# The second mixture layer's loop in program order, with the repeats of its first blocks behind it

## The chip, the cores and the metric

The kernel runs on one core of one Trainium2 chip. The metric is the device time of one execution in microseconds (us), of which the median of several runs counts. Five engines run side by side, each with its own queue of instructions: TensorE (PE in the profile, its weight loads PEld), VectorE (DVE), ScalarE (ACT), GpSimd (POOL) and SyncE (SP), which here issues transfers. TensorE's clock has two levels, 1.2 and 2.4 GHz; the profile gives the granted share of full speed.

## What is computed

Sparse attention (the 32 largest scores of each row), then a first mixture layer of dense form (`moe`), then a second one (`moe2`), in which each token goes to one of eight experts:

```python
logits = x @ w_gate + modality_bias[modality_id]
e_idx = np.argmax(logits, axis=1)
...
gate_w = probs[np.arange(N), e_idx]
for e in range(E):
    mask = e_idx == e
    ...
    h = np.maximum(x[mask] @ w1[e], 0.0)
    out[mask] = gate_w[mask, None] * (h @ w2[e])
```

N is 2304 tokens, D 512, F 1024. The change touches the second mixture layer alone.

## The kernel before

*Tiles.* The tokens are sorted by expert into blocks of 128, 18 of them (NBLK) where all blocks are full, with room for 25 (NSLOT). `gather` fetches the 128 rows of a block from device memory by an indirect transfer that GpSimd issues. `blk_x` turns them on TensorE (four transposes into one bank of PSUM, tile px) and splits them into a higher part bxh (ScalarE) and a lower part bxl (VectorE). `mm1` multiplies by the first weight: two halves of 512 columns, 12 matmuls each (three for each of four chunks: higher by higher, lower by higher, higher by lower), and ScalarE writes each half to hid. `blk_h` does for hid what blk_x does for x, in two quarters of four transposes (tiles pht, bhh, bhl). `mm2` has 24 matmuls of 512 columns, three for each of eight chunks; ScalarE scales the result by the gate (bo), and GpSimd issues the indirect transfer that scatters it to the output.

*Weights.* One expert's weights are held at a time, as a higher and a lower part (e1h, e1l; e2h, e2l). `split` makes them from a raw copy: ScalarE the higher parts, VectorE the lower ones, every third chunk by GpSimd (line 1615); four chunks for the first weight, eight for the second. `cond_split` (line 1681) stands before each block of the loop for each weight: it loads a flag from the table `meta` into a register of each queue and, if the block is the first of a new expert, splits the raw copy and loads the next expert's. In this input two experts occur, so each weight is split twice: once for the first expert, and once inside the loop.

*Stages.* The first three blocks (NPRE) are made of the first three sequences' tokens, before the whole routing is known, and run at the end of the first layer. For each of them meta0 says whether the block was not full; then the block is made again with all tokens (`late_block`, with splits where an expert changes). These three repeats stand as tests ahead of the loop (lines 1724 to 1730). The loop (1732) runs over blocks 3 to 17. Behind it stands a test for blocks above 18 (1750), and the test of `missed`, which repeats the whole kernel exactly (1763). In this input none of these bodies is run.

*Order.* The first layer is put in order by a planner of the kernel's own and emitted with a manual schedule. The second layer is left to the framework's scheduler, which orders each engine's instructions by a simulated time line. A test (`tc.If`) is a branch in each engine's queue: a load of the value into a register, a compare-and-branch, and, where the queues join again, waits on events.

*PSUM.* The pool psX holds px, and pht for the first three blocks; psH holds the two halves of mm1; psY two banks for mm2. When the first layer's pool closes, psX2 takes its two banks, both for pht.

Of the kernel before, what the change touches and what calls it, by code (L numbers as in the profile page):

```python
# [151 lines left out]
def moe_chain_kernel(  # L152
# [159 lines left out]
    def whole(redo):  # L312
# [1287 lines left out]
        two = [ep, 1, psX]  # L1600
# [9 lines left out]
        def split(which):  # L1610
            raw, (h, l) = raws[which - 1], (W1, W2)[which - 1]
            n = raw.shape[1]
            for c in range(n):
                A.activation(h[:, c, :], raw[:, c, :], AF.Copy)
                eng = G if c % 3 == 2 else V
                eng.tensor_tensor(l[:, c, :], raw[:, c, :], h[:, c, :].bitcast(F32), op=OP.subtract)
# [10 lines left out]
        def blk_x(i):  # L1627
            xg = XG.pop(i)
            ps = psX.tile([128, NDC, 128], F32, name="px")
            for c in range(NDC):  # L1630
                PE.transpose(ps[:, c, :], xg[:, c * 128:(c + 1) * 128], ident)
            xh = two[0].tile([128, NDC, 128], F32R, name="bxh", bufs=2)
            xl = two[0].tile([128, NDC, 128], F32R, name="bxl", bufs=2)
            A.activation(xh, ps, AF.Copy)  # L1634
            V.tensor_tensor(xl, ps, xh.bitcast(F32), op=OP.subtract)  # L1635
            X[i] = (xh, xl)
# [13 lines left out]
        def blk_h(i):  # L1650
# [3 lines left out]
            for a in range(NF2 // 4):  # L1654
                ps = two[-1].tile([128, 4, 128], F32, name="pht", bufs=two[1])
# [4 lines left out]
            HT[i] = (hh, hl)  # L1660

        def mm2(i):
            hh, hl = HT.pop(i)
            ps = psY.tile([128, DM], F32, name="py")
            seq = [(x, w, c) for c in range(NF2) for x, w in ((hh, W2[0]), (hl, W2[0]), (hh, W2[1]))]
            for n, (x, w, c) in enumerate(seq):
                PE.matmul(ps, x[:, c, :], w[:, c, :], start=(n == 0), stop=(n == len(seq) - 1))  # L1667
# [12 lines left out]

        def cond_split(i, which):
            f = nc.values_load(meta[0:1, 0, i:i + 1], min_val=0, max_val=1)  # L1682
            with tc.If(f > 0):  # L1683
                split(which)
                load_raw(which, e_value(meta[0:1, 1, i:i + 1]))

# [31 lines left out]
        for i in range(NPRE, NPRE + 3):  # L1718
            gather(i)
        raws[1] = mp.tile([128, NF2, DM], F32, name="raw2")  # L1720
        load_raw(1, e_value(meta[0:1, 1, 0:1]))
        load_raw(2, e_value(meta[0:1, 1, 0:1]))
        blk_x(NPRE)
        for i in range(NPRE):
            f = nc.values_load(meta0[0:1, i:i + 1], min_val=0, max_val=1)
            with tc.If(f > 0):
                if i:
                    cond_split(i, 1)
                    cond_split(i, 2)
                late_block(i)  # L1730
        cond_split(NPRE, 1)
        for i in range(NPRE, NBLK):
            if i > NPRE:
                blk_h(i - 1)
# [12 lines left out]
        cond_split(NBLK - 1, 2)  # L1747
        mm2(NBLK - 1)
        more = nc.values_load(meta[0:1, 2, NBLK:NBLK + 1], min_val=0, max_val=NSLOT)  # L1749
        with tc.If(more > NBLK):  # L1750
            for i in range(NBLK, NSLOT):
                nbl = nc.values_load(meta[0:1, 2, i:i + 1], min_val=0, max_val=NSLOT)
                with tc.If(nbl > i):
                    cond_split(i, 1)
                    cond_split(i, 2)
                    late_block(i)
# [3 lines left out]

    whole(False)
    again = nc.values_load(missed, min_val=0, max_val=1)
    with tc.If(again > 0):
# [31 lines left out]
```

## Time and profile before

| | us |
|---|---|
| median of 3 runs | 1018.72 (1018.18 to 1021.07) |
| the profiled execution | 1023.0 |
| its span, first to last instruction | 1021.1 |
| TensorE busy in the span | 924.2 (91%) |
| VectorE busy | 752.5 (74%) |
| ScalarE busy | 699.3 (68%) |
| GpSimd busy | 548.6 (54%) |

The profile is of one execution; its times are counted from the first instruction of the span. The first layer ends at some 765 us, the first three blocks of the second layer at 809.5, and the loop's last matmul starts at 1009.1. A row of the timeline has start, length (merged rows: of all together), engine, line, operation, tiles written and read, and in brackets the idle time of the engine before it with what ended it. An engine's name with a q (PEldq, ACTq) is its queue: loads of registers, branches and event waits, in which the engine itself does nothing. A row of a line's instructions has the count, the shortest, median and longest length in ns, and the first and last start.

### The profile page before, as it was taken

How to read it: one execution, taken by the hardware profiler on the slowest of the kernel's cores; microseconds unless marked ns; L12 is line 12 of the kernel's file. 1: busy time of each engine (PE TensorE's matmuls, PEld its weight loads, DVE VectorE, ACT ScalarE, POOL GpSimd, SP SyncE). 2: the span in 40 equal slices, each digit the busy share in tenths (PEclk: the TensorE clock that was granted, in tenths of full speed). 3: DMA queues.
4: the chain of work that ended last, by engine and by line, in shares of the span. 5: the costliest groups of instructions: out<-in, count | busy, mean ns of one | idle time of the engine just before them, and what ended most of it. 6: DMA issues, size and time to landing. Idle time of an engine off the chain costs nothing. (4 is left out here: it accounts for less than half of the span.)

```text
span 1021.1 us, 21954 instructions
## 1 busy us (share of the span) xinstructions
PE 924.2 (91%) x7518; PEld 769.0 (75%) x7518; DVE 752.5 (74%) x2510; ACT 699.3 (68%) x1624; POOL 548.6 (54%) x831
## 2 busy tenths in 40 slices
PE   5357599999999999999999999998899899989995
PEld 4245478887778888778888887875797678768883
DVE  7999989999999999999989999996327111331110
ACT  7889889899888999888989888765432222432221
POOL 4678568787767786776876776654210211221000
PEclk8568689999999999999999999998899899989998
DMA  7743230132201123000001000000301521241000
GB/s 188 209 133 108 66 95 16 32 92 66 77 14 33 41 46 100 7 17 30 17 20 40 29 10 2 27 1 9 122 13 53 197 63 42 73 157 50 25 22 27
DMA packets 83795, 60.48 MB, mean 59 GB/s; under 512 B 67009, under 2 KB 67009, under 8 KB 83650
## 3 DMA queue, kind: packets, MB, share of 16 engines
q1 hardware_dynamic: 80770, 49.32, 17.0%
q0 software_dynamic: 2880, 9.44, 2.7%
q8 instruction: 65, 1.06, 0.4%
q14 instruction: 80, 0.66, 0.2%
HBM read 49.30 MB, written 9.44 MB: 58 GB/s over the span
## 5 line engine op out<-in xcount | busy, mean ns | idle before, releaser
L828 DVE MAX8 tk<-wk 128x8 f32<-128x288 f32 x576 | 237.2, 446 | 0.0
L876 POOL TENSOR_TENSOR ss<-mk,ss 128x576 f32<-128x576 bf16 x144 | 185.7, 1297 | 45.5 <-ACT mk L874 44.8
L835 DVE MATCH_REPLACE8 wk<-tk,wk 128x288 f32<-128x288 f32 x432 | 188.2, 441 | 0.0
L874 ACT ACTIVATE mk<-ss,kb 128x576 bf16<-128x576 f32 x144 | 110.6, 780 | 19.2 <-POOL kb L777 19.0
L1647 ACT ACTIVATE hid<-ph 128x512 f32<-128x512 f32 x36 | 21.5, 598 | 140.5 <-PE ph L1646 140.5
L882 ACT ACTIVATE ss<-ss,kb 128x576 f32<-128x576 f32 x144 | 112.0, 779 | 2.8 <-POOL ss L876 2.6
L751 PE MATMUL s<-ks,qt 128*128 128x288 f32 x512 | 95.1, 330 | 19.6 <-ACT ss L762 19.6
L762 ACT ACTIVATE ss<-s 128x576 f32<-128x576 f32 x144 | 93.8, 651 | 21.5 <-PE s L751 20.5
L820 DVE TENSOR_TENSOR wk<-s,ss 128x576 f32<-128x576 f32 x144 | 102.7, 744 | 5.6 <-ACT ss L762 5.6
L946 POOL TENSOR_SCALAR ss<-ss,r,nil 128x576 f32<-128x576 f32 x116 | 95.5, 828 | 17.0 <-DVE r L936 12.5
L1671 POOL DMA_INDIRECT out_dram<-bo,tab x18 | 18.3, 1016 | 158.0 <-ACT bo L1670 150.6
L899 PE MATMUL t<-ident,ss 128*128 128x128 f32 x576 | 89.3, 285 | 10.2 <-ACT ss L882 8.9
L1635 DVE TENSOR_TENSOR bxl<-px,bxh 128x512 fp32r<-128x512 f32 x18 | 12.4, 690 | 115.6 <-ACTq L1683 97.5
L751 PEld LDWEIGHTS s<-ks,qt 128*128 128x128 f32 x512 | 78.2, 208 | 23.9 <-ACT ss L762 21.7
L903 ACT ACTIVATE pt<-t 128x512 f32<-128x512 f32 x144 | 84.3, 597 | 12.5 <-PE t L899 11.2
L899 PEld LDWEIGHTS t<-ident,ss 128*128 128x128 f32 x576 | 67.1, 146 | 19.7 <-ACT ss L882 11.7
L967 PE MATMUL m<-pt,v 128*64 128x128 f32 x1024 | 74.8, 291 | 0.0
L967 PEld LDWEIGHTS m<-pt,v 128*64 128x64 f32 x1024 | 58.6, 144 | 11.9 <-issue 11.9
L1088 DVE SCALAR_TENSOR_TENSOR hb<-m,wfac,hb 128x320 f32<-128x320 f32 (+2 forms) x102 | 49.2, 483 | 16.2 <-PE m L1079 14.9
L1646 PE MATMUL ph<-e1h,bxh 128*128 128x512 f32 x144 | 59.5, 413 | 1.2 <-ACT bxh L1634 0.7
L1667 PE MATMUL py<-e2h,bhh 128*128 128x512 f32 x144 | 58.4, 406 | 1.4 <-ACT bhh L1658 1.4
L832 DVE MAX8 tk<-wk 128x8 f32<-128x288 f32 x144 | 58.6, 442 | 0.0
(309 smaller groups left out, 2672.4 us busy)
## 6 DMA issues: line engine op xcount, KB each, us to landing
raw<-in_moe_w_dram SPq DMA_DIRECT2D x6, 2048.0 KB, 9.6
raw<-in_moe_w_dram SPq DMA_DIRECT2D x18, 512.0 KB, 4.1
kraw<-in_v_dram SPq DMA_DIRECT2D x16, 288.0 KB, 3.9
qraw<-in_q_dram SPq DMA_DIRECT2D x64, 64.0 KB, 2.0
kraw<-in_k_dram SPq DMA_DIRECT2D x32, 128.0 KB, 2.6
v<-in_v_dram SPq DMA_DIRECT2D x32, 128.0 KB, 2.7
x_rows<-row SPq DMA_DIRECT2D x16, 256.0 KB, 2.1
raw<-in_moe_w_out_dram SPq DMA_DIRECT2D x6, 512.0 KB, 4.4
```

The lines of the kernel that those rows point to most:

```text
L751: PE.matmul(ST[u][:, hf, t, :HALF], qt[:, i, :], KS[bat(u), p][:, hd, k0:k0 + HALF], start=(n == 0), stop=(n == len(parts) - 1))
L762: A.activation(SS[u][:, :, hf * HALF:(hf + 1) * HALF], ST[u][:, hf, :, :HALF], AF.Copy)
L820: V.tensor_tensor(WK[u][:, :, w, :], ST[u][:, 0, :, :HALF], SS[u][:, :, HALF:S], op=op)
L828: V.max(TK[u][:, t, r * 8:r * 8 + 8], WK[u][:, t, 0, :])
L835: add("DVE", 426, lambda: V.match_replace(WK[u][:, t, 0, :], TK[u][:, t, r * 8:r * 8 + 8], WK[u][:, t, 0, :], NEG), [tk_at(u, (t, r))], [w ...
L874: A.activation(box["m"], SS[u][:, t, :], AF.Relu, bias=KTH[u][:, t, 1:2], scale=-BIG)
L876: add("POOL", 1250, lambda: G.tensor_tensor(SS[u][:, t, :], box["m"], SS[u][:, t, :], op=OP.subtract), [M], rows_at(u, t))
L882: A.activation(SS[u][:, t, :], SS[u][:, t, :], AF.Exp, bias=KTH[u][:, t, 0:1], scale=-scale * UP, accum_out=SUM[u][:, t:t + 1])
L899: PE.transpose(t[:, c, :], SS[u][:, i, c0:c0 + 128], ident)
L903: A.activation(o, box["t"], AF.Copy)
L946: add("POOL", 790, lambda: G.tensor_scalar(SS[u][:, t, :], SS[u][:, t, :], RR[u][:, t:t + 1], nil, op0=OP.mult, op1=OP.add), [at("r", u, N ...
L967: PE.matmul(ps[hd * 64:(hd + 1) * 64, 0, :], vt[:, c, hd, :], PT[u, hd][:, c, :], start=False, stop=(c == KC - 1), skip_group_check=True)
```

## The change

- `split` puts all lower parts on VectorE.
- `blk_x` uses two banks in turn: px in psX and px2 in psX2. pht has one bank instead of two.
- The whole part from the gathers ahead of the loop to the last mm2 is emitted under a manual schedule of all five engines: each engine issues these instructions in program order.
- The loop is written out anew. Each iteration has mm1 of block i, the gather of block i+3, the test for the first weight of i+1, the first half of mm2 of block i-1, the first quarter of blk_h of i, the second half of mm2 of i-1, the second quarter of blk_h, blk_x of i+2, and the test for the second weight of i. A flag loaded for the first weight's test is kept for the second's.
- The three repeats ahead of the loop go behind it, into the test for further blocks, which now asks for either. Ahead of the loop one test is left (meta0 of the third block), which holds splits alone.
- The value of `missed` is loaded in the loop's last iteration.

```diff
-        two = [ep, 1, psX]
+        two, px = [ep, 1, psX], [(psX, "px")]
...
-                eng = G if c % 3 == 2 else V
-                eng.tensor_tensor(l[:, c, :], raw[:, c, :], h[:, c, :].bitcast(F32), op=OP.subtract)
+                V.tensor_tensor(l[:, c, :], raw[:, c, :], h[:, c, :].bitcast(F32), op=OP.subtract)
...
-            ps = psX.tile([128, NDC, 128], F32, name="px")
+            pool, nm = px[i % len(px)]
+            ps = pool.tile([128, NDC, 128], F32, name=nm)
...
-        def blk_h(i):
+        def blk_h(i, between=None):
...
-            for a in range(NF2 // 4):
-                ps = two[-1].tile([128, 4, 128], F32, name="pht", bufs=two[1])
+            HT[i] = (hh, hl)
+
+            def quarter(a):
+                ps = two[-1].tile([128, 4, 128], F32, name="pht")
...
-            HT[i] = (hh, hl)
-
-        def mm2(i):
-            hh, hl = HT.pop(i)
+            for a in range(NF2 // 4):
+                quarter(a)
+                if a == 0 and between:
+                    between()
+
+        def mm2_first(i):
+            hh, hl = HT[i]
...
+            half = len(seq) // 2
+
+            def go(k):
+                for n in range(k * half, (k + 1) * half):
+                    x, w, c = seq[n]
+                    PE.matmul(ps, x[:, c, :], w[:, c, :], start=(n == 0), stop=(n == len(seq) - 1))
+            go(0)
+            return ps, go
+
+        def mm2(i, first=None):
+            ps, go = first or mm2_first(i)
+            go(1)
...
         def cond_split(i, which):
-            f = nc.values_load(meta[0:1, 0, i:i + 1], min_val=0, max_val=1)
+            f = FLAG[i] if i in FLAG else nc.values_load(meta[0:1, 0, i:i + 1], min_val=0, max_val=1)
+            FLAG[i] = f
...
-        blk_x(NPRE)
-        for i in range(NPRE):
-            f = nc.values_load(meta0[0:1, i:i + 1], min_val=0, max_val=1)
-            with tc.If(f > 0):
-                if i:
+        px.append((two[-1], "px2"))
+        E = mybir.EngineType
+        with tc.manual_schedule(engines={E.PE, E.Activation, E.DVE, E.Pool, E.SP}):
+            for i in range(NPRE, NPRE + 3):
+                gather(i)
+            raws[1] = mp.tile([128, NF2, DM], F32, name="raw2")
+            load_raw(1, e_value(meta[0:1, 1, 0:1]))
+            load_raw(2, e_value(meta[0:1, 1, 0:1]))
+            blk_x(NPRE)
+            early = nc.values_load(meta0[0:1, NPRE - 1:NPRE], min_val=0, max_val=1)
+            with tc.If(early > 0):
+                for i in range(1, NPRE):
                     cond_split(i, 1)
                     cond_split(i, 2)
-                late_block(i)
-        cond_split(NPRE, 1)
-        for i in range(NPRE, NBLK):
-            if i > NPRE:
-                blk_h(i - 1)
-            if i + 1 < NBLK:
-                blk_x(i + 1)
-            if i > NPRE:
-                cond_split(i - 1, 2)
-            mm1(i)
-            if i + 1 < NBLK:
-                cond_split(i + 1, 1)
-            if i > NPRE:
-                mm2(i - 1)
-            if i + 3 < NBLK:
-                gather(i + 3)
-        blk_h(NBLK - 1)
-        cond_split(NBLK - 1, 2)
-        mm2(NBLK - 1)
-        more = nc.values_load(meta[0:1, 2, NBLK:NBLK + 1], min_val=0, max_val=NSLOT)
-        with tc.If(more > NBLK):
+            FLAG.clear()
+            blk_x(NPRE + 1)
+            cond_split(NPRE, 1)
+            for i in range(NPRE, NBLK):
+                mm1(i)
+                if i + 3 < NBLK:
+                    gather(i + 3)
+                if i + 1 < NBLK:
+                    cond_split(i + 1, 1)
+                first = mm2_first(i - 1) if i > NPRE else None
+                blk_h(i, lambda: mm2(i - 1, first) if first else None)
+                if i + 2 < NBLK:
+                    blk_x(i + 2)
+                if i + 1 == NBLK:
+                    more = nc.values_load(meta[0:1, 2, NBLK:NBLK + 1], min_val=0, max_val=NSLOT)
+                    if not redo:
+                        again.append(nc.values_load(missed, min_val=0, max_val=1))
+                cond_split(i, 2)
+            mm2(NBLK - 1)
+        with tc.If(early + more > NBLK):
...
+            with tc.If(early > 0):
...
+                for i in range(NPRE):
+                    f = nc.values_load(meta0[0:1, i:i + 1], min_val=0, max_val=1)
+                    with tc.If(f > 0):
+                        if i:
+                            redo_block(i)
+                        else:
+                            late_block(i)
...
+    again = []
     whole(False)
-    again = nc.values_load(missed, min_val=0, max_val=1)
-    with tc.If(again > 0):
+    with tc.If(again[0] > 0):
         whole(True)
```

## Rows read from the trace of the kernel before

**Rows 1.** Windows: us; busy (count) of PE, PEld, DVE, ACT, POOL; clock, DMA share, GB/s
```profile
834.00:858.60 24.60, 24.60 (x122) 20.49 (x121) 3.96 (x6) 6.70 (x12) 3.99 (x4) 1.00 0.13 44
...
812.85:818.38 5.53, 5.53 (x15) 4.53 (x16) 0.69 (x1) 0.60 (x1) 1.97 (x2) 0.50 0.18 52
...
905.20:910.54 5.34, 5.34 (x15) 4.36 (x16) 1.14 (x2) 0.00 (x0) 0.97 (x1) 0.50 0.89 292
```

**Rows 2.** Timeline of TensorE where the loop begins
```profile
812.85 1.09 PE L1631 MATMUL px<-ident,xg 128*128 128x128 f32 x4 [3.33 <-PEq L1682]
```

**Rows 3.** Timeline at the first weight's switch; then lines 1616 and 1646
```profile
881.35 3.90 ACT L1614 ACTIVATE e1h<-raw 128x1024 fp32r<-128x1024 f32 x4 [4.86 <-PE ph L1646]
...
882.44 2.36 DVE L1616 TENSOR_TENSOR e1l<-raw,e1h 128x1024 fp32r<-128x1024 f32 x2 [7.38 <-ACT e1h L1614]
...
885.28 2.82 DVE L1616 TENSOR_TENSOR e1l<-raw,e1h 128x1024 fp32r<-128x1024 f32 x1 [0.48 <-ACT e1h L1614]
...
885.78 0.66 PE L1657 MATMUL pht<-ident,hid 128*128 128x128 f32 x4 [0.91 <-ACT hid L1647]
...
L1616 POOL TENSOR_TENSOR e1l<-raw,e1h x2: 2636/2676/2715, 714.6 to 884.4; 128x1024 fp32r<-128x1024 f32 x2
...
L1646 PE MATMUL ph<-e1h,bxh x144: 387/389/776, 766.3 to 1000.3; 128*128 128x512 f32 x144
```

**Rows 4.** Timeline at the second weight's switch
```profile
897.99 4.27 ACT L1614 ACTIVATE e2h<-raw 128x512 fp32r<-128x512 f32 x8
...
905.20 1.11 PE L1631 MATMUL px<-ident,xg 128*128 128x128 f32 x4 [3.66 <-DVE bxl L1635]
```

**Rows 5.** Timeline of TensorE in mm2 of the last block
```profile
1003.24 0.49 PE L1667 MATMUL py<-e2h,bhh 128*128 128x512 f32 x1 [0.71 <-ACT bhh L1658]
...
1004.30 0.39 PE L1667 MATMUL py<-e2l,bhh 128*128 128x512 f32 x1
...
1009.09 0.39 PE L1667 MATMUL py<-e2l,bhh 128*128 128x512 f32 x1
```

**Rows 6.** TensorE's queue at the tests: lines 1725, 1726 and 1683
```profile
L1725 PEldq TENSOR_LOAD <-meta x3: 310/312/487, 805.7 to 810.8; - x3
...
L1726 PEldq EVENT_SEMAPHORE  x5: 51/51/51, 809.6 to 811.8; - x5
...
L1726 PEldq COMPARE_BRANCH  x3: 219/334/353, 806.3 to 811.2; - x3
...
L1683 PEldq COMPARE_BRANCH  x32: 70/202/350, 812.5 to 998.7; - x32
```

**Rows 7.** Timeline of one blk_x: transposes, higher part, lower part
```profile
806.16 0.60 PE L1631 MATMUL px<-ident,xg 128*128 128x128 f32 x4
...
806.80 0.60 ACT L1634 ACTIVATE bxh<-px 128x512 fp32r<-128x512 f32 x1 [2.37 <-PE px L1631]
...
807.43 0.69 DVE L1635 TENSOR_TENSOR bxl<-px,bxh 128x512 fp32r<-128x512 f32 x1 [2.28 <-ACT bxh L1634]
```

**Rows 8.** GpSimd's queue: the load of the last test's value, line 1762
```profile
L1762 POOLq TENSOR_LOAD <-missed x1: 297/297/297, 1014.8 to 1014.8; - x1
```

**Rows 9.** Timeline of TensorE after a wait in the first layer; the window behind it
```profile
682.16 0.30 PE L1079 MATMUL m<-xh,w3h 128*128 128x320 f16 x1 [1.56 <-DVE hb L1088]
...
682.20:686.00 3.80, 3.80 (x30) 3.00 (x30) 3.80 (x18) 1.45 (x3) 0.30 (x1) 1.00 0.00 0
```

**Rows 10.** Timeline of GpSimd, gathers and an output; the gathers' issue to landing
```profile
793.91 0.99 POOL L1622 DMA_INDIRECT xg<-x_rows,tab  x1 [3.26 <-DVE gcol L1473]
795.20 0.95 POOL L1622 DMA_INDIRECT xg<-x_rows,tab  x1 [0.30 <-issue]
...
810.58 0.99 POOL L1671 DMA_INDIRECT out_dram<-bo,tab  x1 [6.35 <-ACTq L1726]
...
xg<-x_rows,tab POOLq DMA_INDIRECT x18, 3.4
```

More of the change, by code (lines that the diff above doesn't have):

```diff
@@ L1659, in blk_h @@
                 V.tensor_tensor(hl[:, 4 * a:4 * a + 4, :], ps, hh[:, 4 * a:4 * a + 4, :].bitcast(F32), op=OP.subtract)
-            HT[i] = (hh, hl)
-        def mm2(i):
-            hh, hl = HT.pop(i)
+            for a in range(NF2 // 4):
[4 more added lines that the diff above has]
+            hh, hl = HT[i]
             ps = psY.tile([128, DM], F32, name="py")
             seq = [(x, w, c) for c in range(NF2) for x, w in ((hh, W2[0]), (hl, W2[0]), (hh, W2[1]))]
-            for n, (x, w, c) in enumerate(seq):
-                PE.matmul(ps, x[:, c, :], w[:, c, :], start=(n == 0), stop=(n == len(seq) - 1))
+            half = len(seq) // 2
[8 more added lines that the diff above has]
+            go(1)
+            HT.pop(i)
             o = two[0].tile([128, DM], F32, name="bo", bufs=two[1])
@@ L1679, in late_block @@
             mm2(i)
+        FLAG = {}
         def cond_split(i, which):
-            f = nc.values_load(meta[0:1, 0, i:i + 1], min_val=0, max_val=1)
+            f = FLAG[i] if i in FLAG else nc.values_load(meta[0:1, 0, i:i + 1], min_val=0, max_val=1)
+            FLAG[i] = f
             with tc.If(f > 0):
@@ L1685, in cond_split, with redo_block @@
                 load_raw(which, e_value(meta[0:1, 1, i:i + 1]))
+        def redo_block(i):
+            FLAG.clear()
+            cond_split(i, 1)
+            cond_split(i, 2)
+            late_block(i)
         for i in range(2):
@@ L1717, in whole @@
         two[:] = [mp, 2, main.enter_context(tc.tile_pool(name="psX2", bufs=1, space=PSUM, side="right"))]
[L1718 to L1722, printed above, removed]
-        blk_x(NPRE)
-        for i in range(NPRE):
-            f = nc.values_load(meta0[0:1, i:i + 1], min_val=0, max_val=1)
-            with tc.If(f > 0):
-                if i:
+        px.append((two[-1], "px2"))
@@ L1746, in whole @@
-        blk_h(NBLK - 1)
-        cond_split(NBLK - 1, 2)
-        mm2(NBLK - 1)
-        more = nc.values_load(meta[0:1, 2, NBLK:NBLK + 1], min_val=0, max_val=NSLOT)
-        with tc.If(more > NBLK):
+            FLAG.clear()
+            blk_x(NPRE + 1)
[14 more added lines that the diff above has]
+                        again.append(nc.values_load(missed, min_val=0, max_val=1))
+                cond_split(i, 2)
@@ L1753, in whole @@
                 with tc.If(nbl > i):
-                    cond_split(i, 1)
-                    cond_split(i, 2)
-                    late_block(i)
+                    redo_block(i)
+            with tc.If(early > 0):
+                e0 = e_value(first_e)
+                load_raw(1, e0)
+                load_raw(2, e0)
+                split(1)
+                split(2)
+                e1 = e_value(meta[0:1, 1, 0:1])
+                load_raw(1, e1)
+                load_raw(2, e1)
+                for i in range(NPRE):
+                    f = nc.values_load(meta0[0:1, i:i + 1], min_val=0, max_val=1)
+                    with tc.If(f > 0):
+                        if i:
+                            redo_block(i)
+                        else:
+                            late_block(i)
         main.close()
```

## Prediction, made before the changed kernel was run

> **What bounds the kernel now.** I read three views, in this order: the table of windows by stage, to see which engine is full in the second layer; the timeline of TensorE in the windows that are not full, to see each idle stretch and its releaser; and the single lines behind those releasers. In the steady part of the loop TensorE is busy 24.60 of 24.60 us, two blocks, at the full clock level of 2.4 GHz, while ScalarE and VectorE need 6.70 and 3.96 us [rows 1]. So a block costs about 12.3 us whatever the other engines do, and another order of the same matmuls gains nothing there. Time can only come from stretches in which TensorE stands, or runs at 1.2 GHz because it stood just before. There are four such places, all of them near what the change edits:
>
> - Where the loop begins TensorE idles 3.33 us [rows 2], and then runs 5.53 us at granted clock 0.50 [rows 1]: 2.76 us more than at full clock.
> - At the switch of the first weight it idles 0.91 us [rows 3].
> - At the switch of the second weight it idles 3.66 us [rows 4], and then runs 5.34 us at 0.50 [rows 1]: 2.67 us.
> - In the last block it idles 0.71 us [rows 5].
>
> **The change, part by part.**
>
> *The start of the loop.* Before, three tests of meta0 stand here, each with a whole late block behind it. TensorE's queue had issued everything by 805.7, when the first load of line 1725 runs; the first branch follows at 806.3, and the next thing in the queue is an event wait at 809.6 [rows 6]. The idle stretch begins at 812.85 - 3.33 = 809.52 [rows 2], so that wait ended when the last matmul did: the join after a body that holds matmuls waits for TensorE's own work. Only then come two more loads and branches and the first of line 1682. After the change the one test in front of the loop holds splits alone, which have no TensorE instruction. The 32 tests of that kind before (line 1683) show branches on TensorE's queue, of 202 ns median, and no event wait there [rows 6]. So the queue can go on at 806.3, about 3 us ahead of the matmuls, and needs one load and branch more. I take the whole 3.33 us as gone, and with it the 2.76 us of slow clock. From the other side: had these two tests to run in the open, they would cost two thirds of what three cost after the drain (809.6 to 812.85, 3.25 us), 2.2 us, and might keep the slow clock: 4.9 us. I take zero, because the queue had the lead already and only the drain took it away. What is late next is the first block's own input: its transposes start at 806.16 and its lower part is ready at 807.43 + 0.69 = 808.12 [rows 7], before 809.52. Its new bank (px2) is shown nowhere; it lies in the two banks of the closed pool, and since the old chain used the shared bank, an earlier start is the only other outcome. Gain 6.1 us (1.2 to 6.1).
>
> *A wait that program order adds in the first block.* pht has one bank now. Quarter 1 of blk_h can only be transposed when quarter 0 has been copied and subtracted: 1.96 us from the start of four such transposes to the end of the subtraction (806.16 to 808.12), of which the transposes fill 0.60 [rows 7]. In the first block nothing lies between the quarters: 1.4 us idle (0 to 2). Queued behind that wait on TensorE are blk_x of block 5 and mm1 of block 4. In the 14 later blocks the second half of mm2 lies there: 12 matmuls at (1009.09 - 1004.30)/21 = 0.228 us are 2.74 us [rows 5], more than 1.4. Cost zero, with 0.8 us for the queue to issue four transposes, four more, a branch (0.2 us) and mm1. If that lead is too short I allow 0.3 us a block, 4.2 in all; below zero is excluded, since TensorE is full there.
>
> *The switch of the first weight.* Before, ScalarE began e1h at 881.35, within mm1. Now the second hid of that block stands ahead of it, and behind e1h and e1l stand bhh and bhl of quarter 0, which quarter 1 waits for. From the end of mm1: hid until about 0.8 (0.2 to see the matmul, 0.60 as for a copy of that size [rows 7]), e1h from 1.0, the first e1l 1.09 behind it [rows 3] at 2.1, four e1l on VectorE of 2.36/2 = 1.18 each to 6.8, bhl 0.69 to 7.5. TensorE has 2.74 + 0.4 + 2.74 = 5.9 us of work meanwhile. So it waits 1.6 us where it waited 0.91 (bounds 0.9 and 2.8, the latter were ScalarE 1.2 later). The split by VectorE alone helps: its chunk beside GpSimd's took 2.82 us against 1.18, and GpSimd's own 2.64 to 2.72 [rows 3]. The third chunk no longer waits for that.
>
> *The switch of the second weight.* Before, the transposes of the next x waited for bxl, which was queued on VectorE behind e2l, and everything on TensorE behind them [rows 4]. Now blk_x comes ahead of the split in program order, two blocks early and with two banks, and the split falls under mm1, 24 matmuls or 5.5 us. e2h takes 4.27 us [rows 4]; eight e2l at half of 1.18 follow each e2h, and end some 8 us after the split's place. The first half of mm2 needs four of them, after 5.5 us; the second half begins 3.1 us later. hid, which ScalarE does behind e2h, is wanted by transposes after the first half. I take all 3.66 + 2.67 = 6.3 us as gone (bounds 3 and 6.3).
>
> *The end.* mm2 of the last block starts with four chunks of quarter 0, long ready, and quarter 1 has their 2.74 us against 1.96: 0.71 us gone. The load of `missed` on GpSimd's queue, 297 ns on the way from the last output to the end, is done earlier [rows 8]: 0.3.
>
> *Edits that cost nothing.* The flag kept in a register halves the loads of line 1682 on every queue; they ran ahead of the work. Gathers go out one mm1 earlier, and nothing on GpSimd is behind them but outputs of two blocks ago. SP loads its flags in place; after the switch no load of weights is awaited. The split of the first expert's weights also moves to VectorE: GpSimd's e1l began at 714.6, and the first matmul that reads it starts at 766.3 [rows 3]; 50 us cover it. Three chunks more on VectorE are at most 3 x 1.18 = 3.5 us; what that may shift either way in the first layer is at most this.
>
> *Sum.* Gone: 3.33 + 2.76 + 0.91 + 3.66 + 2.67 + 0.71 + 0.30 = 14.3 us. Added: 1.4 + 1.6 = 3.0. Net 11.3 us. The profiled execution took 1023.0 us, so by it 1011.7; the median of the runs, 1018.72, is 4.3 lower, and with the same distance the forecast is **1007.4 us**. If neither wait showed it would be 1004.4.
>
> **Rivals.**
>
> *The clock falls at the two new waits.* For: idle stretches of 3.33 and 3.66 us were each followed by the low level [rows 1, 2, 4]. Against: 1.56 us of idle before 682.16 left the clock at 1.00 in the stretch behind it [rows 9], and the new waits are 1.4 and 1.6. One fall costs 2.7: 1010.1; both 1012.8.
>
> *The start stays in the open.* The tests in front of the loop are not run ahead: 4.9 us of the gain stay away, 1012.3. This is also the case in which the change doesn't do there what it says.
>
> *The gathers slip.* In the program order of the new block three gathers come first. Before, they ran from 793.91 on, ahead of the last output of the first three blocks at 810.58 [rows 10]. If they were kept behind that output, x would land at 810.58 + 1.0 + 0.3 + 3.4 = 815.3, and mm1 begin some 1.4 us later, 7 us after 809.9, with 2.7 of slow clock: 1017.1, no change. Against: the order of this block binds its own instructions, and the tables they wait for are ready at 793.9.
>
> *The single bank makes every block wait, and the result is slower.* If what lies between the quarters is too little, because bhh and bhl come later than 2.74 us after their transposes, TensorE stops once in each of 14 blocks. The break-even is 11.3/14 = 0.8 us a block, that is bhl 2.0 us later than rows 7 give. A stop that also brought the low clock would cost 2.7 a block more than itself: 1007.4 + 14 x 2.7 = 1045. Against: 1.96 us, and ScalarE and VectorE are idle two thirds of the block [rows 1].
> The Trainium skill has this as a rule (TensorE: Matmul & The Clock Gate, A second HAM failure mode: psum-queue depth-cycling): where a kernel cycles through its PSUM banks in each iteration, the short idle times between groups of matmuls make the clock go up and down, and throughput falls. By it the sum would be that 1045. The trace of before doesn't show it: with two pht banks and one px bank TensorE had no idle time to cycle on, and its clock in the loop is 1.00.
>
> **How the numbers follow.** Chances: forecast as it stands (1004 to 1009.5) 0.50; one or two falls of the clock 0.17; start in the open 0.12; gathers slip 0.09; a wait in every block 0.07; the rest, a first layer that is ordered otherwise, 0.05. The range takes in the first three, with 0.3 us a block and the 1004.4 less some shift of the first layer: 1003 to 1013. A measurement of this kernel can tell about 0.3%, 3.1 us, from no change: faster is under 1015.7. Slipped gathers end within 0.3%, the wait in every block above it, and the rest is divided as 0.03, 0.01, 0.01: faster 0.82, within 0.3% 0.10, slower 0.08.
>
> **What would show it.** In the new profile: no event wait on TensorE's queue and no idle stretch over 1 us before the first mm1 of the loop; one wait of about 1.4 us on bhl between the first block's quarters; one of about 1.6 us on bhl at the first weight's switch; none at the second, and e2h under mm1; the clock at 1.00 from 810 to the last matmul; the last matmul some 11 us earlier; blocks 12.3 us apart. The prediction fails if blocks are further apart than that, if the clock falls inside the loop, or if the first layer ends at another time than 809.5.

## The result, and the profile after

The changed kernel takes 1030.95 us (median of 4 runs, 1029.36 to 1031.97) against 1019.38 for the kernel before (4 runs, 1018.18 to 1021.07): a ratio of 1.0111, interval 1.0089 to 1.0132. It is slower by 1.1%, where the forecast was 1007.4 and faster.

The profiled execution took 1029.36 us, its span 1027.4 (before 1023.0 and 1021.1). Three stretches make up the 6.3 us between the two spans. From the span's start to the loop's first mm1 it is 7.87 us shorter (813.59 to 805.72), the loop 12.11 longer, and what follows the last matmul 2.03 longer (11.65 to 13.68). The medians differ by more, 11.6 us, since the profiled execution before was 3.6 us above its median and the one after 1.6 below.

First the windows of the kernel before from the loop's first mm1 to the end of its last matmul (columns as in [rows 1]), then the same of the changed kernel, with two blocks of the steady part, and a stretch behind the second weight's switch.

```profile
813.59:1009.48 195.89, 189.87 (x894) 155.93 (x892) 39.45 (x53) 56.91 (x100) 31.33 (x29) 0.97 0.17 58
```

```profile
805.72:1013.72 208.00, 190.76 (x892) 152.24 (x892) 38.50 (x56) 58.20 (x99) 26.56 (x27) 0.99 0.16 56
...
834.00:860.68 26.68, 25.19 (x121) 20.31 (x120) 3.96 (x6) 6.91 (x12) 3.98 (x4) 1.00 0.12 41
...
902.90:905.78 2.88, 2.88 (x7) 2.31 (x8) 0.96 (x2) 0.00 (x0) 0.00 (x0) 0.50 0.17 42
```

The second row is the one to set beside 24.60 of 24.60 in [rows 1]: two blocks now need 26.68 us, and TensorE is idle in 1.49 of them, at full clock. The idle stretches of TensorE in the loop, by what ended them (us in total, times, longest):

```profile
PE ph L1646 <- ACT hid L1647: 13.1, 15, 2.7
PE pht L1659 <- DVE bhl L1661: 2.9, 2, 1.7
PE py L1676 <- ACTq L1702: 1.2, 1, 1.2
PE ph L1646 <- ACTq L1702: 0.9, 1, 0.9
```

The first line is new, and it comes 15 times: once for each block of the loop. The timeline of the changed kernel in two blocks that follow one another shows what it is:

```profile
831.61 0.39 PE L1646 MATMUL ph<-e1l,bxh 128*128 128x512 f32 x1
832.10 0.60 ACT L1647 ACTIVATE hid<-ph 128x512 f32<-128x512 f32 x1 [2.04 <-PE ph L1646]
...
832.75 0.50 PE L1646 MATMUL ph<-e1h,bxh 128*128 128x512 f32 x1 [0.75 <-ACT hid L1647]
...
833.09 0.40 PE L1646 MATMUL ph<-e1h,bxl 128*128 128x512 f32 x1
...
846.12 0.50 PE L1646 MATMUL ph<-e1h,bxh 128*128 128x512 f32 x1 [0.75 <-ACT hid L1647]
```

The matmul of 831.61 is the last of mm1's first half. ScalarE copies that half out of PSUM from 832.10 to 832.70, and only then, at 832.75, does the second half of the same mm1 start, though it writes another bank. Both halves are one tile (`ph`, NH2 x 512), and the second half waits for the reader of the first. The blocks stand 846.12 - 832.75 = 13.37 us apart. Beside the 0.75 of idle, some 0.3 go where the matmuls no longer overlap (833.09 - 832.75 = 0.34 in place of 0.23, and an end that is not covered).

The tile was one tile before, too. The timeline of the kernel before, in the one block of its loop where the halves stood close together, shows a wait that fits it:

```profile
818.42 0.40 PE L1646 MATMUL ph<-e1l,bxh 128*128 128x512 f32 x1
...
818.65 0.60 PE L1631 MATMUL px<-ident,xg 128*128 128x128 f32 x4
818.85 0.60 ACT L1647 ACTIVATE hid<-ph 128x512 f32<-128x512 f32 x1 [4.22 <-PE ph L1646]
...
819.50 0.50 PE L1646 MATMUL ph<-e1h,bxh 128*128 128x512 f32 x1 [0.25 <-ACTq L1683]
```

Four transposes lie between the halves, and the second starts 0.05 us after the copy ends (818.85 + 0.60 = 819.45). The releaser that is named is another one: ScalarE's queue passing the test of line 1683, which it does right behind that copy. So the row can't tell whether the matmul waited for the copy or for the test, and the waits' table has it under the test. In the steady part of the loop before, the first half ended at 838.9, and four transposes and twenty matmuls of mm2 followed it; the second half started at 843.77, and the copy had long been done.

The other places that the prediction went through, in the timeline of the changed kernel: the loop's start, the first block, the first weight's switch, the second weight's, and the last block.

```profile
805.72 0.50 PE L1646 MATMUL ph<-e1h,bxh 128*128 128x512 f32 x1 [0.93 <-ACTq L1702]
...
814.86 0.33 PE L1659 MATMUL pht<-ident,hid 128*128 128x128 f32 x1 [1.69 <-DVE bhl L1661]
...
882.96 0.33 PE L1659 MATMUL pht<-ident,hid 128*128 128x128 f32 x1 [1.23 <-DVE bhl L1661]
...
898.09 4.27 ACT L1614 ACTIVATE e2h<-raw 128x512 fp32r<-128x512 f32 x8
...
902.25 0.59 ACT L1647 ACTIVATE hid<-ph 128x512 f32<-128x512 f32 x1
...
902.90 0.80 PE L1646 MATMUL ph<-e1h,bxh 128*128 128x512 f32 x1 [2.74 <-ACT hid L1647]
...
1007.77 0.50 PE L1676 MATMUL py<-e2h,bhh 128*128 128x512 f32 x1 [1.23 <-ACTq L1702]
```

At the second weight's switch the same shared tile costs more: the copy stands behind eight e2h on ScalarE, the second half waits 2.74 us for it, and the clock is at 0.50 from then to 905.78 (the window above).

Added up over the loop: 195.9 us before; less the slow clock after its start ((818.38 - 813.59)/2 = 2.4) and the waits of [rows 3 to 5] with the other slow stretch of [rows 1] (0.91 + 3.66 + 0.71 + 2.67 = 7.95); plus 13.1 of idle in the 15 second halves and 15 x 0.29 behind them (17.5), half of 2.88 at low clock (1.4), and 1.69 + 1.23 + 1.23. That gives 208.6, and 208.0 is measured.

### The profile page after: what moved, and what is told of

It reads as the page before. It is cut to its first block, busy times and chain, and to the rows that moved or that the text cites. A ratio compares the mean times of both kernels' runs of the same rounds, so it can differ in the third digit from the quotient of the medians.

```text
span 1027.4 us, 21742 instructions
## 1 busy us (share of the span) xinstructions
PE 919.6 (90%) x7518; PEld 761.1 (74%) x7518; DVE 751.9 (73%) x2516; ACT 699.9 (68%) x1624; POOL 537.1 (52%) x825
## 5 line engine op out<-in xcount | busy, mean ns | idle before, releaser
L828 DVE MAX8 tk<-wk 128x8 f32<-128x288 f32 x576 | 237.7, 447 | 0.0
L1661 DVE TENSOR_TENSOR bhl<-pht,bhh 128x512 fp32r<-128x512 f32 x36 | 24.9, 690 | 167.7 <-ACT bhh L1660 165.0
L1099 POOL TENSOR_TENSOR hl<-hb,hh 128x320 f16<-128x320 f32 (+2 forms) x54 | 36.3, 673 | 48.2 <-ACT hh L1094 47.8
L1079 PE MATMUL m<-xh,w3h 128*128 128x320 f16 (+2 forms) x204 | 56.3, 281 | 3.2 <-DVE hb L1088 2.8
```

What stands on the lines that cost most here:

```text
L828: V.max(TK[u][:, t, r * 8:r * 8 + 8], WK[u][:, t, 0, :])
```

## The experiments

Theory: the halves of mm1 share a tile, and the order written out puts them back to back. The first rival is that another edit, the split on VectorE, the single pht bank or the repeats' new place, carries the loss. Each ratio is to the kernel before, in runs on the same chip.

**The shared tile taken away.** The changed kernel with one tile for each half:

```diff
-            ps = psH.tile([128, NH2, 512], F32, name="ph")
             for hf in range(NH2):
+                ps = psH.tile([128, 512], F32, name=f"ph{hf}")
...
-                    PE.matmul(ps[:, hf, :], x[:, c, :], w[:, c, fs], start=(n == 0), stop=(n == len(seq) - 1))
-                A.activation(hid[:, fs], ps[:, hf, :], AF.Relu)
+                    PE.matmul(ps, x[:, c, :], w[:, c, fs], start=(n == 0), stop=(n == len(seq) - 1))
+                A.activation(hid[:, fs], ps, AF.Relu)
```

> The changed kernel with the two halves of mm1 in two PSUM tiles (ph0, ph1) instead of one tile of two banks. Theory: in program order the second half's first matmul waits until ScalarE has emptied the first half, because the two halves are one tile; 0.75 us idle and about 0.25 us of restart in each of 15 blocks, and 2.74 us idle with 1.4 us of slow clock at the second weight's switch. Then blocks stand 12.3 us apart instead of 13.37, no idle stretch before a second half is left, and the time is 1031 - 15 - 4 = 1012 us (1009 to 1015). Rival A: TensorE waits there for something else (program order itself, ScalarE reading PSUM while TensorE writes): blocks stay 13.3 us apart, 1031. Rival B: the wait goes but the next one takes its place (quarter 0 of blk_h on hid): half of the gain, 1022.

Measured: 1011.49 us, ratio 0.9913 (0.9880 to 0.9946), 19.5 less than the changed kernel. Its table of waits for TensorE in the loop, and the window of the whole loop:

```profile
PE pht L1659 <- DVE bhl L1661: 2.9, 2, 1.7
PE py L1676 <- ACTq L1702: 1.2, 1, 1.2
PE ph L1646 <- ACTq L1702: 0.9, 1, 0.9
```

```profile
806.77:995.89 189.12, 184.95 (x892) 152.28 (x892) 38.48 (x56) 58.22 (x99) 26.57 (x27) 1.00 0.18 61
```

The line of 15 waits is gone, with that of the second weight's switch in it; the others stand as they were, to the tenth. Blocks are 12.29 us apart, and the loop takes 189.12 us in place of 208.00: 18.9 of the 19.5 us are in the loop. That is also what the rows of the changed kernel add up to (13.1 of idle, 15 x 0.29 and 1.4).

**The order taken away, the tile kept.** The changed kernel with the first half of mm2 between the halves of mm1:

```diff
-        def mm1(i):
+        def mm1(i, between=None):
...
+                if hf == 0 and between:
+                    between()
...
-                mm1(i)
+                got = []
+                mm1(i, lambda: got.append(mm2_first(i - 1)) if i > NPRE else None)
+                first = got[0] if got else None
...
-                first = mm2_first(i - 1) if i > NPRE else None
```

> The changed kernel with ph as one tile, but the first half of mm2 of the block before stands between the two halves of mm1 instead of behind them. Theory: the wait of the second half is still in the program, and 2.74 us of matmuls cover its 0.75 us: blocks 12.3 us apart, no idle stretch of 0.75. At the second weight's switch that mm2 now comes 2.7 us earlier and waits for e2l, some 2 to 5 us. Time 1012 to 1018. Rival A (the halves don't wait for each other's tile): 13.3 us a block, 1031.

Measured: 1015.59 us, ratio 0.9962 (0.9946 to 0.9978). Its waits for TensorE in the loop:

```profile
PE pht L1661 <- DVE bhl L1663: 5.6, 2, 4.0
PE py L1678 <- ACTq L1704: 1.2, 1, 1.2
PE ph L1646 <- ACTq L1704: 0.9, 1, 0.9
PE ph L1646 <- ACT hid L1647: 0.7, 1, 0.7
```

One of the 15 is left, the first block's, which has no mm2 to put between. Its price is in the first line: at the first weight's switch the quarter waits 3.95 us instead of 1.23, because the 2.74 us of matmuls that covered the split there have been moved, and the clock is at 0.50 from 883 to 886, behind that wait. The expectation had the price at the second switch, in a wait for e2l; there is none there.

**The wait made longer.** The changed kernel, in which ScalarE makes the copy of the first half twice:

```diff
                 A.activation(hid[:, fs], ps[:, hf, :], AF.Relu)
+                if hf == 0:
+                    A.activation(hid[:, fs], ps[:, hf, :], AF.Relu)
```

> The changed kernel in which ScalarE empties the first half of ph twice (the same copy again, 0.60 us), so that the second half of mm1 is given free 0.6 us later. Theory (the second half waits for the emptying of the first, and TensorE is the engine that everything follows): the 0.75 us wait becomes 1.35 in every block, a block takes 13.9 in place of 13.33, and the fifteen blocks 9 us more: 1040 (1038 to 1042). The clock shows whether a longer idle per block brings it down: with 1.35 us idle in 13.9 it stayed at 1.00, or each fall adds some 3 us and the time passes 1045. Rival (the wait is not for that copy): 1031 to 1033, with the wait still 0.75.

Measured: 1040.21 us, ratio 1.0206 (1.0180 to 1.0232), 9.3 above the changed kernel. One block of its timeline, and a window of two blocks:

```profile
838.02 0.60 ACT L1647 ACTIVATE hid<-ph 128x512 f32<-128x512 f32 x1 [1.98 <-PE ph L1646]
838.64 0.60 ACT L1649 ACTIVATE hid<-ph 128x512 f32<-128x512 f32 x1
...
839.29 0.50 PE L1646 MATMUL ph<-e1h,bxh 128*128 128x512 f32 x1 [1.32 <-ACT hid L1649]
```

```profile
834.00:861.90 27.90, 25.27 (x122) 20.35 (x121) 3.96 (x6) 8.11 (x14) 3.98 (x4) 1.00 0.12 38
```

0.75 became 1.32 in the steady blocks, and the clock stayed at 1.00 in them. The wait grows by 0.57 us for a copy of 0.60; ScalarE is busy in 8.11 of 27.90 us and yet sets the pace.

**The hand-written order as a whole.** The changed kernel without its manual schedule, so that the framework's scheduler orders the new loop; all other edits stay, the shared tile too:

```diff
-        with tc.manual_schedule(engines={E.PE, E.Activation, E.DVE, E.Pool, E.SP}):
+        with ExitStack():
```

> The changed kernel with its order written out by hand taken away: the scheduler orders the same loop again, with the repeats still behind it, the split on VectorE alone and ph one tile of two banks. In the built program the scheduler puts the second layer's twelve first matmuls (2.7 us) between the two halves of mm1 in every block, as it did in the kernel before. Theory (the loss is ScalarE emptying ph's first half between halves that stand back to back): the 0.75 us wait is gone from every block, a block takes 12.3 us in place of 13.37, fifteen blocks give 16 us, and with the waits at the start, the first block and the last as in the changed kernel the time is 1011 (1007 to 1016). Rival (the loss is another part of the change: the split, the repeats' place or the single bank for pht): it stays above 1026.

Measured: 1007.89 us, ratio 0.9898 (0.9869 to 0.9927), at the low end of the range. Its timeline of one block, TensorE and ScalarE, and its windows of the whole loop and of two blocks:

```profile
836.45 0.39 PE L1646 MATMUL ph<-e1l,bxh 128*128 128x512 f32 x1
...
839.66 0.39 PE L1676 MATMUL py<-e2l,bhh 128*128 128x512 f32 x1
...
839.88 0.39 PE L1646 MATMUL ph<-e1h,bxh 128*128 128x512 f32 x1
...
836.88 0.60 ACT L1647 ACTIVATE hid<-ph 128x512 f32<-128x512 f32 x1 [4.89 <-PE ph L1646]
```

```profile
807.77:992.17 184.40, 183.46 (x884) 151.52 (x884) 37.95 (x55) 57.81 (x99) 24.19 (x24) 1.00 0.17 60
834.00:858.60 24.60, 24.60 (x122) 20.46 (x121) 3.96 (x6) 6.94 (x12) 3.97 (x4) 1.00 0.13 44
```

The scheduler puts twelve matmuls of mm2 and four transposes between the halves, under which the copy (836.88 to 837.48) lies, and the loop takes 184.40 us. So the other edits together, in the scheduler's order, bring 10.6 us against the kernel before (1018.46 on that chip), and the order written out by hand costs 22 to 23 us as long as the tile is shared.

**The shared tile of the kernel before.** The kernel before with two tiles for ph, and nothing else (the same edit as the first one):

> The kernel before with ph as two tiles. Theory: there the scheduler has 4 transposes and 20 matmuls between the halves, so the one tile costs nothing but 0.25 us once: 1019 (1015 to 1023, since the scheduler may order anew). Rival: the one tile costs something in that kernel too, and the gain of the first experiment has nothing to do with program order: 1009 or less.

Measured: 1007.96 us, ratio 0.9897 (0.9855 to 0.9938). That is a miss of 11 us: I expected nothing, since that order kept the halves apart. With two tiles the scheduler ordered the whole loop otherwise. Both weights' switches and the last block have no wait over 0.45 us, and one place of [rows 2] is left, in its timeline with the window behind it:

```profile
808.73 0.63 PE L1631 MATMUL px<-ident,xg 128*128 128x128 f32 x4 [3.74 <-DVEq L1726]
```

```profile
808.73:815.00 6.27, 6.27 (x31) 5.22 (x32) 0.69 (x1) 1.31 (x3) 1.97 (x2) 1.00 0.30 88
```

What follows is that the waits at the switches, which the prediction laid to the place of the splits, came with the order that the scheduler makes for a shared tile. Which of the scheduler's choices decides isn't settled: its split of the second weight starts at 883.8 instead of 897.99, and the transposes of the rows stand directly behind those of hid.

**Both.** The kernel without manual schedule and with two tiles for ph:

> The kernel of e5 with ph as two tiles of one bank: scheduler's order, repeats behind the loop, split on VectorE alone. If a second tile matters only where halves stand back to back, it gives nothing on top of the scheduler's order but at the W2 switch, and the time is within 4 us of e5's. If what the kernel before lost at its switches also came from the shared tile (it gained 11 us from two tiles), this one is the fastest so far, 1004 (1001 to 1008): the loop of 184.3 us of that run and no wait of 3.7 us at its start.

Measured: 1004.77 us (6 runs, 1003.46 to 1006.60), ratio 0.9870 (0.9846 to 0.9893). It is the fastest of all here, 14 us under the kernel before and 26 under the changed one. All that its TensorE waits for from 795 us on (the first lies in the three blocks ahead of the loop):

```profile
PE py L1676 <- ACT bhh L1660: 0.7, 1, 0.7
PE ph L1646 <- ACT bxh L1634: 0.4, 1, 0.4
PE pht L1659 <- DVE bhl L1661: 0.2, 1, 0.2
```

Against the kernel before with two tiles, the 3.74 us at the loop's start are down to 0.45, now that no repeats stand there. Against the one with the shared tile (1007.89) it gains 3.1, where the two expectations were a gain within 4 us or a time of 1004: both hold by the time. The traces lean to the first: the loop itself takes 184.09 us against 184.40, and the gain lies ahead of it (41.73 us against 44.33 from the first mm1 of the first three blocks to the loop's).

**The parts, one by one.** Two tiles for pht besides, in the hand-written order:

```diff
-        two, px = [ep, 1, psX], [(psX, "px")]
+        two, px, pht = [ep, 1, psX], [(psX, "px")], [psX]
...
-                ps = two[-1].tile([128, 4, 128], F32, name="pht")
+                ps = pht[a % len(pht)].tile([128, 4, 128], F32, name="pht")
...
+        pht.append(two[-1])
```

> The first experiment, and pht in two banks in turn (one in psX, which stands unused in the loop, one in psX2). Theory: the two waits on bhl that the one bank makes go: 1.69 us in the loop's first block and most of 1.23 us at the first weight's switch; 2 to 3 us below the first experiment, 1009 (1006 to 1012). Rival: the waits move on to hid or to e1l and the time is that of the first experiment.

Measured: 1008.77 us, ratio 0.9893 (0.9862 to 0.9923), 2.7 less than with two tiles for ph alone. The intervals of the two overlap; that the gain is this edit's is seen in the trace, where the loop takes 186.19 us in place of 189.12. The waits on bhl are gone; of those over 0.3 us two remain, the two last rows of the view of the first experiment, unchanged. Each is a matmul that waits until ScalarE has passed a test whose body, by the code, would write the matmul's weights. On that kernel, GpSimd's third of the split restored:

```diff
-                V.tensor_tensor(l[:, c, :], raw[:, c, :], h[:, c, :].bitcast(F32), op=OP.subtract)
+                eng = G if c % 3 == 2 else V
+                eng.tensor_tensor(l[:, c, :], raw[:, c, :], h[:, c, :].bitcast(F32), op=OP.subtract)
```

> The changed kernel with two tiles for ph and two for pht (1008.8), and GpSimd taking every third piece of the weights' split again, as in the kernel before: only the split's part of the change is undone. With VectorE alone the last e1l ends at about 874.8 and the first matmul that reads new weights starts at 874.9, so nothing waits; with the third piece on GpSimd (2.8 us against 1.2) it ends within a microsecond of that on either side. Theory: 1008.8, within 2 us. Rival (the split on VectorE alone carries part of the gain or loss): 2 to 4 us off, with a wait before mm1 or before the quarters at the switches.

Measured: 1006.99 us, ratio 0.9887 (0.9857 to 0.9918), the same as without the edit within what the runs can tell. The loop takes 186.48 us against 186.19, so the split's engine is worth nothing there; the 1.8 us between the medians are no more than the stretch behind the last matmul differs between the two profiled executions (15.1 us without the edit, 11.7 with it). And on the same kernel, two tests moved so that ScalarE passes them earlier:

```diff
-            blk_x(NPRE + 1)
             cond_split(NPRE, 1)
+            blk_x(NPRE + 1)
...
-        def mm2(i, first=None):
+        def mm2(i, first=None, then=None):
             ps, go = first or mm2_first(i)
             go(1)
+            if then:
+                then()
...
-                blk_h(i, lambda: mm2(i - 1, first) if first else None)
+                last = (lambda: cond_split(i, 2)) if i + 1 == NBLK else None
+                blk_h(i, lambda: mm2(i - 1, first, last) if first else None)
...
-                cond_split(i, 2)
+                if i + 1 < NBLK:
+                    cond_split(i, 2)
```

> The changed kernel with two tiles for ph and two for pht (1008.8), and two steps moved: the second block's transposes behind the test of the fourth block at the loop's start, and the last block's W2 test ahead of the emptying of py, so that ScalarE passes both tests earlier. Theory (TensorE waits there for ScalarE to have passed a test that its own matmul does not need): the 0.93 us at the start and the 1.24 us ahead of the last block's second layer shrink to under 0.4 each, 1007 (1005.5 to 1008). Rival (TensorE's wait only moves to what ScalarE has next, bxh or bhh): 1008.8 unchanged, with another wait of about a microsecond in the same places.

Measured: 1005.96 us (6 runs, 1005.18 to 1007.43), ratio 0.9880 (0.9857 to 0.9902). Its waits for TensorE, the first from the three blocks ahead of the loop:

```profile
PE py L1676 <- ACT bhh L1660: 0.7, 1, 0.7
PE ph L1646 <- ACTq L1704: 0.4, 1, 0.4
PE pht L1659 <- ACTq L1704: 0.2, 1, 0.2
```

The 0.93 is down to 0.44, and ahead of the last block's mm2 no wait over 0.2 is left of the 1.24. The loop takes 184.24 us, against 184.09 in the fastest kernel: a written-out order can be as fast as the scheduler's, when its waits are known. Last, the second bank for the rows, taken out of the fastest kernel:

```diff
-        px.append((two[-1], "px2"))
```

> The kernel of e6 (1004.8) with the one bank for the rows' transposes that the kernel before had, so that this part of the change alone is undone. The wait of 3.66 us in the kernel before was for this bank, behind ScalarE's eight pieces of W2. Theory A (the second bank is what took that wait away): it comes back at the W2 switch, with half clock behind it, and the time is 1008.5 to 1011. Theory B (with ph in two tiles the scheduler's order puts the transposes where the bank is long empty): 1004.8, within 2 us, and no wait over 0.7 us at that place.

Measured: 1006.78 us (1004.67 to 1009.72), ratio 0.9880 (0.9846 to 0.9914). Its first mm1 of the loop waits 0.9 us for bxh, and no wait of more than 0.2 us stands between that and the end. So in this order the second bank is not needed to keep the wait of 3.66 us away; the kernel before with two tiles for ph, which has one such bank, has no such wait either. In the hand-written order one bank was not tried.

## Why the prediction was wrong

*The step that failed* is in its first part: "a block costs about 12.3 us whatever the other engines do, and another order of the same matmuls gains nothing there". The first half of the sentence was read from one order, in which 24 instructions lay between mm1's halves; it holds only as long as work of 0.75 us or more lies there. I asked of each moved step what hides it, but not of the steps that stayed the same and lost a neighbour. The code says it (one tile of NH2 x 512, a copy for each half), and one place of the trace before fits it (819.50). Price: 15 x 1.04 us, and at the second switch 2.0 more of idle and 1.4 of slow clock; with it taken out the time was 1011.49. The 4.1 us from there to the forecast of 1007.4 are of the size of what the paragraphs below find besides: 0.93 us left at the start, 1.23 at the end, and a tail that is longer instead of shorter.

*The second weight's switch.* Predicted: the 6.3 us gone, bounds 3 and 6.3. Measured: 2.74 of idle and 1.4 of slow clock, so 2.2 gone. That transposes want hid only after mm2's first half was right, but mm1's own second half wanted it first. It is the same step again: without the shared tile the place has no wait.

*The first block and the first weight's switch.* Predicted waits on bhl: 1.4 and 1.6. Measured: 1.69 and 1.23, and none in the other blocks. (The 0.2 us that the second of these sums allows "to see the matmul" is read from no row; the copy above starts 832.10 - 831.61 - 0.39 = 0.10 us after the matmul's end.) The single pht bank costs what the sum said, 2.9 against 3.0; with two banks the loop became 2.9 us shorter.

*The start.* Predicted: no wait and no slow clock. Measured: the clock stayed at 1.00 and 0.93 us of idle were left, for ScalarE to pass the test. The rows of the branches of the tests (line 1702), on TensorE's queue and on ScalarE's, show both halves of it; the first of each is the loop's start:

```profile
L1702 PEldq COMPARE_BRANCH  x32: 70/202/332, 802.0 to 1005.6; - x32
...
L1702 ACTq COMPARE_BRANCH  x32: 38/45/50, 805.2 to 1007.3; - x32
```

TensorE's queue was there at 802.0 and ran ahead, as the prediction said. ScalarE's came at 805.2 and had passed at 805.7, behind the result of the third block and the higher part of the next rows, which the code puts ahead of this test; the matmul started at 805.72. From the first mm1 of the first three blocks (766.28 before, 762.85 after) to the loop's, it is 47.31 - 42.87 = 4.4 us shorter. Two things belong beside that number. The 2.4 us of slow clock behind the loop's first mm1 are gone too. And some 1.7 us of it are no gain of the start: in the profiled execution before, the clock fell to 0.50 among the first three blocks' first matmuls, and after it did not (rows in the last section). 4.4 + 2.4 - 1.7 = 5.1, against 6.1 predicted: what is missing is the 0.93.

*The end.* Predicted: 0.71 gone. Measured: no wait for bhh any more, but 1.23 for ScalarE's last branch (1007.3, behind bo and bhh). The prediction looked at TensorE's queue alone in [rows 6]; it missed ScalarE's in both places.

*The tail.* Predicted 0.3 less; from the last output's issue to the end of the span it was 12.63 us against 10.60, 2.0 more. The load of `missed` did move, but it was worth nothing: GpSimd is through the first of the two tests only about when that output has landed (3.7 us after its issue before, 4.0 after), and the branch of the second starts 4.7 us after the output's issue in both kernels (1010.53 to 1015.2 before, 1014.77 to 1019.5 after). What is longer is the second test itself (below).

*The edits at nothing.* Right: the split by VectorE (a loop of 186.48 us with it undone, 186.19 without). The gathers and the flags show up in no wait, and were not undone by themselves. Not borne out: the second bank for the rows as a reason for the freed second switch.

*The rivals.* The sign came out as in the fourth rival, a wait in every block, with a break-even of 0.8 us a block against 1.04 measured. But its mechanism was another: in the blocks after the first, pht's bank made only the one at the first weight's switch wait, and in the steady blocks the clock had no part in it. So the chance of 0.07 was given to the wrong bank. (The clock of 1.00 that the prediction reads for the loop before is that of its steady part; the whole loop has 0.97 in the window above.)
The Trainium skill's rule that was weighed there (TensorE: Matmul & The Clock Gate, A second HAM failure mode: psum-queue depth-cycling) tells of a bf16 kernel whose short idle times between groups of matmuls, in each iteration, bring the clock up and down. The runs here don't agree for this loop: with 0.75 us of idle in each 13.4, and with 1.32 in each 13.9, the granted clock of the steady blocks was 1.00.

*What held.* The sum of the other edits. It came to -11.3, and with the order left to the scheduler they brought 1007.89 and a ratio of 0.9898. That it is so near is in part luck: the two waits of 3.0 us that the sum adds don't occur in that order, and the stretch behind the last matmul, which it makes 0.3 shorter, is 2.2 longer (13.83 us against 11.65). And since the kernel before reached the same time by two tiles alone, that agreement doesn't prove the sum's terms one by one: only the start's (3.74 us against 0.45) is shown apart.

*What stays open.* Why the profiled executions before and after differ by 6.3 us and the medians by 11.6: the stretch before the second layer differs from one profiled execution to the next (its first mm1 began between 762.6 and 767.3 in the twelve kernels, which differ little up to there), and no run here tells why.

## What to carry over

Before an order is written out by hand, list for each tile of several banks who reads its first part, and what stood between the parts in the scheduler's order: in this framework a part that is to be written waits for the readers of the whole tile. One tile for each bank takes no more PSUM and gave 19.5 us in the hand-written order, where it took the wait away, and 11 in the scheduler's, where it changed the order.
The Trainium skill (PSUM — Partial Sum Buffer, Summary: rules for kernel authors) says to read another bank than the one that a matmul writes, and to guard by bank. The trace agrees (with two tiles the 13.1 us of these waits are gone), but the banks must be separate tiles for the waits to follow it.
An engine that is busy a quarter of the time (6.91 of 26.68 us) can still set the pace, if its short step stands between two matmuls that nothing separates. And where a test's body writes what a matmul reads, the matmul can wait for another engine to pass that test, though the body is not run (ScalarE here, 0.93 and 1.23 us): put the test where that engine gets to it early.

## What the runs showed of the chip

How long TensorE waits did not tell whether its clock fell. In the kernel before, 3.33 us at the loop's start were followed by 0.50 [rows 1, 2], and so were 2.74 at the second switch of the changed kernel. In the kernel before with two tiles, 3.74 us at the same place as [rows 2] were followed by 1.00 (window 808.73 to 815.00 above). And the same short waits at the start of the first three blocks, 0.69 and 0.40 us on the same releasers, were followed by 0.50 in the profiled execution before and by 1.00 in the one after. The timeline of TensorE and a window behind the waits, before and then after:

```profile
766.28 0.49 PE L1646 MATMUL ph<-e1h,bxh 128*128 128x512 f32 x1 [0.69 <-ACT bxh L1634]
...
768.00:770.00 2.00, 2.00 (x7) 1.61 (x6) 1.29 (x7) 0.60 (x1) 0.00 (x0) 0.50 0.24 92
```

```profile
762.85 0.49 PE L1646 MATMUL ph<-e1h,bxh 128*128 128x512 f32 x1 [0.69 <-ACT bxh L1634]
...
764.00:766.00 2.00, 2.00 (x12) 1.70 (x11) 1.66 (x9) 0.60 (x1) 0.00 (x0) 1.00 0.44 131
```

The price of 2.7 us that the prediction put on each fall is thus not a rule: the falls read here cost from 1.4 us (2.88 at 0.50) to 2.8 (5.53 at 0.50), and the wait's length alone doesn't say whether one comes. A gain that consists of a fall that stays away is as uncertain.

A test whose body is not run cost GpSimd very different times at the span's end, with the same instructions. The rows of its event waits behind the last branch, in the changed kernel and in the one with mm2 between the halves:

```profile
L1803 POOLq EVENT_SEMAPHORE  x6: 17/30/43, 1022.1 to 1024.7; - x6
L1803 POOLq COMPARE_BRANCH  x1: 45/45/45, 1019.5 to 1019.5; - x1
```

```profile
L1806 POOLq EVENT_SEMAPHORE  x6: 17/30/43, 1010.2 to 1010.6; - x6
L1806 POOLq COMPARE_BRANCH  x1: 45/45/45, 1007.5 to 1007.5; - x1
```

Both need 2.6 to 2.7 us from the branch to the first event wait; from the first to the last it is 2.6 in one and 0.4 in the other, and the profile shows nothing that the longer one waits for. The 2 us are most of the tail's difference: 12.63 from the last output to the end, and 10.74. In the other kernels the stretch was 0.4 or 0.5 (the kernel before with one tile and with two, the three kernels of the new loop in the scheduler's order, GpSimd's third restored) or 2.5 to 2.7 (the copy made twice, two tiles for ph, two for pht, the tests moved). So medians of kernels that differ by 2 us or less may differ by this and not by their loops. The bodies that are jumped over and the place of the code differ between kernels; what it is was not tried.
